# Projection tiles cut into 64-row halves ahead of the attention loop, with five score maxima threaded between them

## The chip, the cores and the metric

The kernel runs on one core of one Trainium2 chip. The metric is the device time of one execution in microseconds; the median of three executions is compared. All tensors are float32, and the matmuls read their operands as float32r.

## The reference

`x` has 2048 rows of 512. It is normalised along its rows, and the normalised rows feed an attention block with 32 heads of 16 columns and a two-layer block with a squared ReLU. The silu of the second gates the first, and `x` is added.

```python
xn  = layernorm(x)                                   # 2048 x 512
qkv = xn @ wqkv                                      # 512 x 1536: q, k, v of 32 heads
p   = softmax(q k^T / 4)                             # per head, 2048 x 2048
s   = (p @ v) @ wo
h   = relu(xn @ w1 + b1) ** 2                        # 1792 columns
out = x + s * silu(h @ w2 + b2)
```

## The kernel before

**Number format.** Every operand is kept as a high and a low part, and a product is three matmuls: high by high, high by low, low by high (`terms3`, L262). A projection tile, 128 by 512 outputs over 512 contracted columns, is therefore 4 pieces of 128 rows times 3, that is 12 matmuls of 128 rows, all adding into one PSUM bank.

**Three stages.** First the layer norm, the transposes of `x`, and the projection tiles of the first heads. Then, from L1109 on, a stage that is called "lead" here: it works off the remaining projection tiles (list `rest`, each entry a generator that `pump` at L1025 advances matmul by matmul) and beside them computes row maxima of the scores. Then the loop (L1332) over 32 units, each four heads by 512 queries, in 16 steps of 128 keys, 512 steps in all. It holds the exponentials, the product with v, the two-layer block, `wo`, and what is left of the maxima.

**Maxima.** The softmax subtracts the maximum of each row of scores. `max_mm(j)` (L288) computes one piece: a matmul of 64 rows (the head's 16 columns are stored as a high, high, low layout within 64 partitions; j is the half of the array, partitions 0 to 63 or 64 to 127) at L300 into a PSUM bank, and a reduction on VectorE at L308 that leaves the maximum of 512 columns. There are 2048 pieces in all, 64 to each of 32 units. Each must be made once, either in the lead or in the loop. Pieces are made by turns on the two halves, since a matmul of 64 rows fills half the array and one on each half run beside each other. In the lead a piece takes its bank alternately from the pool `pe` (tile `se`, three banks) and the pool `pm` (tile `pm_t`, three banks); in the loop from `pm` alone.

**A round of the lead.** L1109 to L1148 run one round for each tile: six pieces of maxima (three on each half), then twelve full matmuls (`pump(12, 1)`). Since `pump(60, 1)` at L1103 stops in the middle of a tile, each twelve are the last eleven of one tile and the first of the next. When a tile is done, ScalarE copies its bank to `raw` (L954) or to `vt` (L971), GpSimd splits `raw` into `hl` (L80, L81), and SyncE stores `hl` to q_d or k_d (L912) in HBM. The tiles' own banks alternate between the single banks of `pd` and `pv` (`q_bank`, L925). `hl` has three buffers and `raw` two. In the same rounds the normalised `x` (xn_d, 1 MB each), keys (ka), queries (qm, qe) and v are moved between HBM and SBUF.

**The order of the work.** The order on TensorE, ScalarE, VectorE and GpSimd is that in which the program issues; TensorE takes its matmuls in that order for both halves. `max_end` (L314) follows the maxima: when 9/16 and 11/16 of a unit's pieces are done it asks for the next unit's queries.

**The loop.** `long_slots` (L1251) runs two steps at a time in a "visit": 12 units of the two-layer block on one half, 8 exponential scores (L1161) and some maxima, and 8 matmuls of 128 rows by 32 columns for the product with v (`pv_mm`, L374), which come four to a step. A visit has two forms. If `ahead_m` (L1241) finds that the maxima are ahead of their due time, it holds 7 maxima and the product of both steps at its end (L1283); otherwise 8 maxima, with the first step's product moved between the tenth and the eleventh unit (L1290, L1295).

```python
                if ahead_m(sum(done_m) + 7, st + 2):
                    visit(h, "s" + "D" * 12 + "s", ".mmsmssmsmssmm")
                    ...
                else:
                    visit(h, "D" * 10, "msmsmsmsms")
```

Of the kernel before, what the change touches and what calls it, by code (L numbers as in the profile page):

```python
# [31 lines left out]
SHIFT = 8  # L32
NVT = 7
# [6 lines left out]
def kernel(  # L40
# [55 lines left out]
    with ExitStack() as ph:  # L96
# [217 lines left out]
        def max_end():  # L314
            while steps[0] < sum(done_m) // 4:
                u, s = divmod(steps[0], 16)
                if s == 15 and min(done_m) < 32 * (u + 1):
                    return
                steps[0] += 1
                if s in (9, 11) and u + 1 < NU:  # L320
                    assert min(done_m) >= 32 * u + 16
# [611 lines left out]
        def qk_tile(m, c, last=False):  # L933
            ps = pd.tile([P, 512], F32, name="pd_t") if last else q_bank()
            for out_, lh, rh, first_, last_ in qk_terms(m, c, ps):
                nc.tensor.matmul(out_, lh(slice(0, P)), rh(slice(0, P)), start=first_, stop=last_)  # L936
                if not last_:
                    yield
            if last:
# [6 lines left out]
                yield  # L946
                return
# [9 lines left out]
            yield  # L957

        def v_tile(c, tt):
            xT = xTs[c]  # L960
            ps = q_bank()
            ts_ = slice(tt * P, (tt + 1) * P)
            for out_, lh, rh, first_, last_ in terms3(ps, [
                (lambda a, q, ko=ko: xT[q, a, ko, ts_], lambda b, q, ko=ko: wa_t[q, b, ko, 2 * P :])
                for ko in range(KO)
            ]):
                nc.tensor.matmul(out_, lh(slice(0, P)), rh(slice(0, P)), start=first_, stop=last_)  # L967
                if not last_:
                    yield
            vt = vts[(4 * c + tt) % NVT]  # L970
            nc.scalar.activation(  # L971
                vt[:, :, :DH], ps.rearrange("p (h d) -> p h d", d=DH), AF.Copy
            )
            nc.sync.dma_start(v_d[:, c * 4 + tt, :], vt.rearrange("p h d -> p (h d)"))
            lead[1] += 1
            yield
# [48 lines left out]
        def pump(n, keep=0):  # L1025
            for _ in range(n):
                while True:
                    todo = ahead or rest
                    if todo is rest and len(rest) <= keep:
                        return  # L1030
                    if next(todo[0], todo) is not todo:
# [25 lines left out]
        for i in range(NT + 3):  # L1057
# [21 lines left out]
            if i >= 3 and (i - 3) % 4 == 3:  # L1079
                c = (i - 3) // 4  # L1080
                ahead.append(qk_tile(4, c))
                (rest if c else ahead).append(qk_tile(0, c))
                rest += [v_tile(c, tt) for tt in range(4)]
# [14 lines left out]
        for n in (2, 3):  # L1098
            fill_ring("ka", n, 1.0)
        rest += [  # L1100
            qk_tile(m, c, (m, c) == (7, 3)) for c in range(4) for m in (1, 5, 2, 6, 3, 7)
        ]
        pump(60, 1)  # L1103
        warm = const.tile([P, 1], F32, name="warm")
# [3 lines left out]
        b = 0  # L1108
        while len(rest) > 1:  # L1109
            now[0] = b - 100  # L1110
            shift_due()
            for _ in range(3):
                for j in range(2):
                    max_mm(j, True)
            pump(12, 1)
# [32 lines left out]
            b += 1  # L1148
        m0[0] = sum(done_m)
# [236 lines left out]
```

## Time and profile before

| what | value |
|---|---|
| median of 3 runs | 1689.39 us (1685.15 to 1689.98) |
| the profiled execution | 1685.93 us |
| its span, first to last instruction | 1684.1 us |
| TensorE busy | 1645.7 us, 98% of the span |
| VectorE busy | 1334.7 us, 79% |
| ScalarE busy | 1190.0 us, 71% |
| first piece of the maxima starts | 64.92 us |
| first exponential score starts (the loop) | 200.11 us |

A matmul's row in the timeline gives its start and a modelled end; matmuls are pipelined, so the time that one takes from the next is the distance of their starts, not the duration. The same holds for VectorE's reductions. A row ahead of which TensorE waited names what ended the wait in brackets. "64*128" in a matmul's row means 64 rows by 128 columns of the array.

### The profile page before, as it was taken

Reading aid. Unit: us, or ns where it says so; the run is one execution under the profiler, and the core shown is the slowest. Engines: PE = TensorE matmul, PEld = TensorE weight load, DVE = VectorE, ACT = ScalarE, POOL = GpSimd, SP = SyncE. Lnnn points to the kernel's source line nnn. Section 1 sums busy time; section 2 is a strip of 40 time slices with the busy share of each in tenths; the row PEclk is TensorE's granted clock in tenths of the full one; section 3 lists DMA queues with packets and bytes.
Section 4 is the critical chain, followed back from the end, with each engine's and each line's share of the span. In section 5 each row is a group of like instructions: output and inputs, shape, how many; then the busy total and the mean of one; then the engine's idle time right before and its main releaser. Section 6 shows DMA issues by size and latency. Waiting matters only on the chain.

```text
span 1684.1 us, 35351 instructions
## 1 busy us (share of the span) xinstructions
PE 1645.7 (98%) x13296; PEld 980.9 (58%) x13296; DVE 1334.7 (79%) x2294; ACT 1190.0 (71%) x2354; POOL 529.2 (31%) x548
## 2 busy tenths in 40 slices
PE   6999999999999999999999999999999999999998
PEld 5766666556655665665566556545655565555533
DVE  6499988887887788777877878888888888888512
ACT  7211277778877777787788777777777777766685
POOL 4424467513311321231133113212221233133333
PEclk9999999999999999999999999999999999999999
DMA  8558465526322533353243324352424332167344
GB/s 282 167 186 258 153 198 157 143 71 158 99 78 78 136 93 84 98 132 80 78 125 114 79 85 117 94 117 68 133 72 108 102 108 67 33 201 213 101 138 134
DMA packets 156723, 208.00 MB, mean 124 GB/s; under 512 B 51272, under 2 KB 71240, under 8 KB 155016
## 3 DMA queue, kind: packets, MB, share of 16 engines
q1 hardware_dynamic: 156552, 205.74, 43.2%
q8 instruction: 105, 1.72, 0.5%
q14 instruction: 66, 0.54, 0.1%
HBM read 149.30 MB, written 56.09 MB: 122 GB/s over the span
## 4 chain that ended last, share of the span: by engine, by line
PE 84%; issue 5%; POOL 4%; DMA 3%; DVE 2%; SPq 1%; ACT 1%; POOLq 0%; ACTq 0%
PE po L374 26%; PE pd_t L234 16%; PE se L1161 14%; PE pm_t L300 13%; PE pd_t L202 5%; PE pd_t L936 2%; PE po L936 2%; DVE mx L308 2%; PE se L300 2%; PE po L967 1%; PE pd_t L967 1%; DMA hl<-r_d 1%; POOL ts L751 1%; POOL ts L750 1%; PE se L936 1%
## 5 line engine op out<-in xcount | busy, mean ns | idle before, releaser
L308 DVE TENSOR_REDUCE mx<-pm_t 128x1 f32<-128x512 f32 x1946 | 1207.3, 683 | 228.7 <-PE pm_t L300 145.3
L1167 ACT ACTIVATE pt<-se 128x512 f32<-128x512 f32 x1721 | 911.6, 614 | 245.0 <-PE se L1161 146.7
L1161 PE MATMUL se<-qe,ka 64*128 64x512 f32 x1988 | 759.5, 420 | 0.1
L300 PE MATMUL pm_t<-ka,qm 64*128 64x512 f32 x1946 | 738.7, 416 | 4.4 <-DVE mx L308 2.7
L374 PE MATMUL po<-pt,v 128*32 128x512 f32 x3562 | 522.2, 602 | 0.0
L300 PEld LDWEIGHTS pm_t<-ka,qm 64*128 64x128 f32 x1946 | 341.8, 184 | 165.7 <-DVE mx L308 150.8
L1161 PEld LDWEIGHTS se<-qe,ka 64*128 64x128 f32 x1988 | 353.2, 184 | 129.8 <-ACT pt L1167 76.8
L234 PE MATMUL pd_t<-xc,w1s 64*128 64x256 f32 x2352 | 318.0, 285 | 0.0
L234 PEld LDWEIGHTS pd_t<-xc,w1s 64*128 64x128 f32 x2352 | 296.8, 187 | 34.6 <-issue 31.8
L234 PE MATMUL pd_t<-w2t,hT 64*128 64x512 f32 x936 | 249.0, 403 | 0.0
L374 PE MATMUL po<-ex,v 128*32 128x512 f32 x534 | 207.9, 601 | 0.0
L1167 ACT ACTIVATE ex<-se 128x512 f32<-128x512 f32 x267 | 159.8, 614 | 46.8 <-PE se L1161 22.7
L234 PEld LDWEIGHTS pd_t<-w2t,hT 64*128 64x128 f32 x936 | 162.4, 185 | 33.9 <-issue 25.1
L374 PEld LDWEIGHTS po<-pt,v 128*32 128x32 f32 x3562 | 90.8, 109 | 155.8 <-issue 138.6
L548 POOL TENSOR_TENSOR r<-r 128x512 f32<-128x512 f32 x49 | 51.0, 1040 | 320.1 <-ACT r L545 320.1
L567 POOL TENSOR_TENSOR u<-u,b_t 128x512 f32<-128x512 f32 x16 | 20.5, 1284 | 283.9 <-ACT u L566 252.2
L202 PE MATMUL pd_t<-w2t,hT 64*128 64x512 f32 x408 | 106.1, 392 | 0.6 <-POOL w2t L81 0.6
L412 POOL TENSOR_TENSOR ot<-ot,hl 128x512 f32<-128x512 f32 x31 | 39.8, 1284 | 211.8 <-DMA hl<-r_d 129.8
L202 PE MATMUL pd_t<-wot,oc 64*128 64x512 f32 x336 | 90.9, 406 | 8.9 <-DVE mx L308 6.2
L202 PEld LDWEIGHTS pd_t<-wot,oc 64*128 64x128 f32 x336 | 58.5, 185 | 57.7 <-ACT pt L1167 16.2
L308 DVE TENSOR_REDUCE mx<-se 128x1 f32<-128x512 f32 x102 | 69.7, 683 | 15.7 <-PE se L300 9.0
L202 PEld LDWEIGHTS pd_t<-w2t,hT 64*128 64x128 f32 x408 | 72.8, 185 | 10.6 <-POOL w2t L81 1.5
(125 smaller groups left out, 1229.2 us busy)
## 6 DMA issues: line engine op xcount, KB each, us to landing
w1s<-w_d SPq DMA_DIRECT2D x196, 256.0 KB
qm<-q_d SPq DMA_DIRECT2D x384, 32.0 KB
qe<-q_d SPq DMA_DIRECT2D x384, 32.0 KB
ka<-k_d SPq DMA_DIRECT2D x96, 128.0 KB
xn_d<-xT SPq DMA_DIRECT2D x8, 1024.0 KB
k_d<-hl SPq DMA_DIRECT2D x32, 256.0 KB
q_d<-hl SPq DMA_DIRECT2D x32, 256.0 KB
xc<-xn_d SPq DMA_DIRECT2D x16, 512.0 KB
```

The costliest lines, as they stand in the source:

```text
L202: mm = nc.tensor.matmul(out_, lh(r), rh(r), start=first_ and lane == 0, stop=last_ and lane == 1, skip_group_check=True,)
L234: mm = nc.tensor.matmul(out_, lh(r), rh(r), start=first_ and lane == 0, stop=last_ and lane == 1, skip_group_check=True,)
L300: nc.tensor.matmul(ps, qms[u][p][64 * j : 64 * j + 64, qb * P : (qb + 1) * P], kas[qd, p][64 * j : 64 * j + 64, kc * 512 : (kc + 1) * 512] ...
L308: return nc.vector.tensor_reduce(mxs[u][:, c, kc : kc + 1], ps, axis=AX.X, op=ALU.max)
L374: nc.tensor.matmul(po[32 * j : 32 * j + 32, :], vs[qd][:, (4 * kb + j) * VW : (4 * kb + j) * VW + 32], pts[j], start=(kb == 0), stop=(kb = ...
L412: nc.gpsimd.tensor_tensor(ot, ot, hl[:, 1].bitcast(F32), op=ALU.mult)
L548: nc.gpsimd.tensor_tensor(r, r, r, op=ALU.mult)
L567: nc.gpsimd.tensor_tensor(u, u, b2_t, op=ALU.add)
L936: nc.tensor.matmul(out_, lh(slice(0, P)), rh(slice(0, P)), start=first_, stop=last_)
L967: nc.tensor.matmul(out_, lh(slice(0, P)), rh(slice(0, P)), start=first_, stop=last_)
L1161: nc.tensor.matmul(se, kas[qd, j // 2][b : b + 64, kb * P : (kb + 1) * P], qes[u][j // 2][b : b + 64, :], start=True, stop=True,)
L1167: return nc.scalar.activation(pts[j], se, AF.Exp, scale=0.25)
```

## The change

Each tile of the lead is issued as two lists: `low`, its 12 matmuls on partitions 0 to 63, and `high`, the same 12 on partitions 64 to 127, both into the same bank. `low` of a tile is issued alternately with what `far` holds at that moment: `far` starts with 23 empty places (15 + LAG), and each tile's `high` is appended to it, so that a tile's second half runs about one tile and eight steps behind its first. Between the twelve of `low` stand two or three maxima of half 0, between those of `high` three or two of half 1: five to a tile where there were six. The empty places of the first two rounds get seven further maxima. After the last tile a tail of steps works off `far`. All maxima of the lead now take their banks from `pm`; the tiles take theirs in turn from `pd`, `pv` and three times `pe`. The first matmul of a second half waits for the reduction of the maximum that ends the first half. The tile that `pump(60, 1)` leaves unfinished is finished, in full matmuls, ahead of the first maximum.

```diff
@@ max_end
+                if s == 11 and min(done_m) < 32 * u + 16:
+                    return
...
         def q_bank():
-            if not lead[0]:
-                return pe.tile([P, 512], F32, name="se")
-            lead[2] += 1
-            if lead[2] % 2:
+            lead[2] += lead[0]
+            if lead[2] % 5 == 1:
                 return pd.tile([P, 512], F32, name="pd_t")
-            return pv.tile([P, 512], F32, name="po")
+            if lead[2] % 5 == 2:
+                return pv.tile([P, 512], F32, name="po")
+            return pe.tile([P, 512], F32, name="se")
...
+        def lead_halves(kind, m, c):
+            ps = q_bank()
+            mms = (v_terms if kind == "v" else qk_terms)(m, c, ps)
+            done = [None]
+
+            def emit(mm, lane, follow):
+                r = slice(64 * lane, 64 * lane + 64)
+                out_, lh, rh, first_, last_ = mm
+                inst = nc.tensor.matmul(
+                    out_, lh(r), rh(r),
+                    start=first_ and lane == 0, stop=last_ and lane == 1,
+                    skip_group_check=True,
+                )
+                if follow:
+                    tc.add_manual_dep(
+                        inst.ins, done[0].ins.name,
...
+                    )
+                if lane and last_:
+                    q_end(kind, m, c, ps)
+
+            def behind(inst):
+                done[0] = inst
+
+            return [
+                [lambda mm=mm, lane=lane: emit(mm, lane, lane and mm is mms[0]) for mm in mms]
+                for lane in range(2)
+            ], behind
...
         pump(60, 1)
+        if not isinstance(rest[0], tuple):
+            for _ in rest.pop(0):
+                pass
...
+        far = [None] * (15 + LAG)
+
+        def step(near):
+            for mine in near:
+                if mine is not None:
+                    mine()
+                if far and far[0] is not None:
+                    far[0]()
+                del far[:1]
+
         while len(rest) > 1:
             now[0] = b - 100
             shift_due()
-            for _ in range(3):
-                for j in range(2):
-                    max_mm(j, True)
-            pump(12, 1)
+            (low, high), behind = lead_halves(*rest.pop(0))
+            low[6:6] = [lambda: max_mm(0)] * (1 + b % 2)
+            low.append(lambda behind=behind: behind(max_mm(0)))
+            high[4:4] = [lambda: max_mm(1)]
+            high[9:9] = [lambda: max_mm(1)]
+            if b % 2 == 0:
+                high.append(lambda: max_mm(1))
+            if b < 2:
+                for i in range(len(far)):
+                    if far[i] is None and i % 5 == 2:
+                        far[i] = lambda: max_mm(1)
+            far += high
+            step(low)
             max_end()
...
+        while far:
+            step([lambda: max_mm(0)] + [None] * 4)
+        max_end()
```

On TensorE, in the middle of the lead (the queries of heads 8 to 15 over the first 512 rows of `x`, the first tile that reads the weights `wr_t`), the program before has a burst of maxima between whole tiles:

```order
L967 MATMUL po<-wa_t,xT_187 128x512 x11
L936 MATMUL pd_t<-xT_188,wr_t 128x512
L300 MATMUL se<-ka_203,qm_202 128x512
L300 MATMUL pm_t<-ka_203,qm_202 128x512
L300 MATMUL se<-ka_203,qm_202 128x512
L300 MATMUL pm_t<-ka_203,qm_202 128x512
L300 MATMUL se<-ka_203,qm_202 128x512
L300 MATMUL pm_t<-ka_203,qm_202 128x512
L936 MATMUL pd_t<-xT_188,wr_t 128x512 x11
```

The same tile (bank `pd_t`) on TensorE in the changed program; a row's shape is that of the output, so the halves read 128x512 as well:

```order
L987 MATMUL se<-wa_t,xT_187 128x512
L987 MATMUL pd_t<-xT_188,wr_t 128x512
L987 MATMUL se<-wa_t,xT_187 128x512
L987 MATMUL pd_t<-xT_188,wr_t 128x512
L301 MATMUL pm_t<-ka_204,qm_201 128x512
L987 MATMUL pd_t<-xT_188,wr_t 128x512
L987 MATMUL se<-wa_t,xT_187 128x512
L987 MATMUL pd_t<-xT_188,wr_t 128x512
L987 MATMUL se<-wa_t,xT_187 128x512
L301 MATMUL pm_t<-ka_204,qm_201 128x512
L987 MATMUL se<-wa_t,xT_187 128x512
L987 MATMUL pd_t<-xT_188,wr_t 128x512
```

Halves of an earlier tile and of this one now alternate, with a single maximum among them here and there, and all maxima name `pm_t`.

In the loop, the end of a visit near step 240 on TensorE, before: the last units of the two-layer block (`pd_t<-xc`), the exponential scores (`se<-qe`), the maxima (`pm_t<-ka`), then the products with v of two steps (`po`) in one run of eight.

```order
L234 MATMUL pd_t<-xc,w1s_2327 128x256 x2
L300 MATMUL pm_t<-ka_203,qm_201 128x512
L234 MATMUL pd_t<-xc,w1s_2327 128x256 x2
L300 MATMUL pm_t<-ka_203,qm_201 128x512
L1161 MATMUL se<-qe_689,ka_685 128x512
L374 MATMUL po<-ex_2307,v_1438 32x512
L374 MATMUL po<-pt_1351,v_1438 32x512
L374 MATMUL po<-pt_1354,v_1438 32x512
L374 MATMUL po<-pt_1343,v_1438 32x512
L374 MATMUL po<-pt_1344,v_1438 32x512
```

At the same place in the changed program:

```order
L235 MATMUL pd_t<-xc,w1s_2632 128x256 x2
L376 MATMUL po<-ex_2610,v_1614 32x512
L376 MATMUL po<-pt_1494,v_1614 32x512
L376 MATMUL po<-pt_1488,v_1614 32x512
L376 MATMUL po<-pt_1490,v_1614 32x512
L235 MATMUL pd_t<-xc,w1s_2632 128x256 x2
L301 MATMUL pm_t<-ka_204,qm_200 128x512
L235 MATMUL pd_t<-xc,w1s_2632 128x256 x2
L301 MATMUL pm_t<-ka_204,qm_200 128x512
L1222 MATMUL se<-qe_688,ka_684 128x512
L1222 MATMUL se<-qe_689,ka_685 128x512 x2
L301 MATMUL pm_t<-ka_204,qm_200 128x512
```

The product of one step has moved into the middle of the block's units: this visit has taken the form with 8 maxima. Counted over the whole order, 27 visits (the 116th to the 142nd pair of steps) change from 7 maxima to 8; the 27 that are missing ahead of the first exponential score, 178 in place of 205, are made up there, and the last maximum stands in the same step as before.

More of the change, by code (lines that the diff above doesn't have):

```diff
@@ L32 @@
 SHIFT = 8
+LAG = 8
 NVT = 7
@@ L1080 @@
                 c = (i - 3) // 4
-                ahead.append(qk_tile(4, c))
-                (rest if c else ahead).append(qk_tile(0, c))
-                rest += [v_tile(c, tt) for tt in range(4)]
+                ahead.append(("qk", 4, c))
+                (rest if c else ahead).append(("qk", 0, c))
+                rest += [("v", tt, c) for tt in range(4)]
         while ahead:
@@ L1100 @@
         rest += [
-            qk_tile(m, c, (m, c) == (7, 3)) for c in range(4) for m in (1, 5, 2, 6, 3, 7)
+            ("qk", m, c) + ((True,) if (m, c) == (7, 3) else ())
+            for c in range(4) for m in (1, 5, 2, 6, 3, 7)
         ]
         pump(60, 1)
+        if not isinstance(rest[0], tuple):
+            for _ in rest.pop(0):
+                pass
         warm = const.tile([P, 1], F32, name="warm")
```

41 lines of the change are left out of this document (22 added, 19 removed).

## The prediction

> **What bounds the kernel now.** I read the page first: it says which engine the span follows.
>
> ```profile
> PE 1645.7 (98%) x13296; PEld 980.9 (58%) x13296; DVE 1334.7 (79%) x2294; ACT 1190.0 (71%) x2354; POOL 529.2 (31%) x548
> ```
>
> TensorE (PE) has work in flight for 98% of the span, VectorE (DVE) for 79%. These are averages over stages with different limits, so the second view is the table by stage, cut at the first maximum (64.92 us) and at the first exponential score (200.11 us).
>
> ```profile
> 64.92:200.11 135.19, 133.53 (x615) 93.08 (x615) 126.32 (x213) 22.42 (x39) 52.76 (x56) 1.00 0.62 199
> 200.11:1600.00 1399.89, 1387.14 (x11997) 817.65 (x12000) 1160.43 (x1959) 1069.94 (x2126) 415.51 (x431) 1.00 0.41 110
> ```
>
> The columns are stretch, length, busy PE, PEld, DVE, ACT and POOL, granted clock, DMA share, GB/s. In the lead (135.19 us) PE and DVE are both nearly full; ScalarE and GpSimd are not; the clock is 1.00, so nothing can come from there. Which of the two sets the pace is seen in one round, in order of time, PE first, then DVE:
>
> ```profile
> 140.52 0.39 PE L936 MATMUL pd_t<-xT,wr_t 128*128 128x512 f32 x1
> 140.83 0.49 PE L300 MATMUL se<-ka,qm 64*128 64x512 f32 x1
> 140.84 0.49 PE L300 MATMUL pm_t<-ka,qm 64*128 64x512 f32 x1
> 141.17 0.39 PE L300 MATMUL se<-ka,qm 64*128 64x512 f32 x1
> ...
> 141.40 0.39 PE L300 MATMUL se<-ka,qm 64*128 64x512 f32 x1
> 141.41 0.39 PE L300 MATMUL pm_t<-ka,qm 64*128 64x512 f32 x1
> 141.72 2.79 PE L936 MATMUL pd_t<-xT,wr_t 128*128 128x512 f32 x11
> 144.35 0.39 PE L936 MATMUL po<-xT,wr_t 128*128 128x512 f32 x1
> 144.67 0.49 PE L300 MATMUL se<-ka,qm 64*128 64x512 f32 x1
> ```
>
> ```profile
> 141.36 0.69 DVE L308 TENSOR_REDUCE mx<-se 128x1 f32<-128x512 f32 x1 [0.16 <-PE pm_t L300]
> 141.97 0.68 DVE L308 TENSOR_REDUCE mx<-pm_t 128x1 f32<-128x512 f32 x1
> ...
> 144.36 0.68 DVE L308 TENSOR_REDUCE mx<-pm_t 128x1 f32<-128x512 f32 x1
> 145.20 0.69 DVE L308 TENSOR_REDUCE mx<-se 128x1 f32<-128x512 f32 x1 [0.16 <-PE pm_t L300]
> ```
>
> The round lasts 144.67 - 140.83 = 3.84 us. A pair of maxima, one on each half of the array, takes as long as one full matmul: 141.40 - 141.17 = 0.23. The eleven full matmuls take 144.35 - 141.72 = 2.63, of which the first takes about 0.34 and the others 0.23. So the round is 15 places of 0.23 (3.45) and about 0.1 extra at each of four **seams**, where the array goes from 128 rows to 64 and back: 140.52 to 140.83 is 0.31, 140.83 to 141.17 is 0.34, 141.41 to 141.72 is 0.31. Together 3.85: PE fills the round without a wait. DVE needs six steps of 0.60 (141.97 to 144.36 is four, 2.39), 3.6 us, and sits idle for the rest, 0.16 of it shown as a wait for PE. **The lead is bound by PE**, with DVE 6% behind it.
>
> **The change part by part: the lead.** A tile becomes 24 halves and 5 maxima, all of 64 rows, so 14.5 pairs instead of 15 places, and the seams go. That holds only if two halves with 512 columns run beside each other as the maxima do. The loop has such pairs (the two-layer block on one half, scores on the other):
>
> ```profile
> 610.38 0.39 PE L234 MATMUL pd_t<-w2t,hT 64*128 64x512 f32 x1
> 610.38 0.39 PE L300 MATMUL pm_t<-ka,qm 64*128 64x512 f32 x1
> 610.61 0.40 PE L234 MATMUL pd_t<-w2t,hT 64*128 64x512 f32 x1
> ...
> 611.99 0.39 PE L234 MATMUL pd_t<-w2t,hT 64*128 64x512 f32 x1
> ...
> 613.07 0.40 PE L234 MATMUL pd_t<-w2t,hT 64*128 64x512 f32 x1
> ```
>
> Seven steps in 611.99 - 610.38 = 1.61 give 0.23; all eleven to 613.07 give 0.245, with waits for other engines in them. I take 0.23 and keep 0.245 as the upper end. The tiles: 33 x 14.5 = 478 steps, and a tail of 24 in which the second half of the last tile is worked off alone: 502 x 0.23 = 115.5 us.
>
> Where it starts:
>
> ```profile
> 63.18 0.86 PE L967 MATMUL se<-wa_t,xT 128*128 128x512 f32 x3
> 64.92 0.46 PE L300 MATMUL se<-ka,qm 64*128 64x512 f32 x1 [0.88 <-DMA ka<-k_d]
> 66.81 0.47 PE L300 MATMUL pm_t<-ka,qm 64*128 64x512 f32 x1 [1.43 <-DMA ka<-k_d]
> ```
>
> Before, PE runs out of projections at about 63.9 and waits for the keys until 66.81. After, the eleven matmuls that are left of the open tile (11 x 0.23 = 2.5) fill that gap; the first maximum comes two steps later, at 66.9. So the steps begin at 66.4, and what was a wait is work that stood behind the burst.
>
> What is added to the 115.5:
>
> ```profile
> 202.54 0.49 PE L300 MATMUL pm_t<-ka,qm 64*128 64x512 f32 x1
> 203.07 1.89 DVE L308 TENSOR_REDUCE mx<-pm_t 128x1 f32<-128x512 f32 x3 [1.14 <-PE se L1161]
> 203.81 0.50 PE L300 MATMUL pm_t<-ka,qm 64*128 64x512 f32 x1 [0.31 <-DVE mx L308]
> 203.82 0.50 PE L1161 MATMUL se<-qe,ka 64*128 64x512 f32 x1
> ```
>
> *Waits for a bank.* All maxima now share three banks. These rows show a bank's turn: 203.81 - 202.54 = 1.27 us from matmul to matmul. The order gives ten maxima in 29 steps, at steps 3, 6, 8, 13, 13, 18, 20, 21, 27, 28; the third one after any stands at least 7 steps (1.6 us) later, and ten reductions take 6.0 of the 6.7 us. Worked through place by place, waits are left in the first two rounds, which hold seven extra maxima (1.6 us), and in the tail (0.7): with the rest 2.5 us. The rows also show what a wait costs: the score on the other half (203.82) starts only with the maximum. By the Trainium skill ("TensorE: Matmul & The Clock Gate", section "Step-by-step: what each phase is for") only weight loads are pulled ahead, and "the MATMULs themselves stay in program order". These rows agree; were it otherwise, the other half would run on, and the 2.5 would be nothing.
>
> *Unit ends.* Two of these fall in the lead, each a transpose for the shift:
>
> ```profile
> L335 PE MATMUL pm_t<-ident,m 128*16 128x128 f32 x4 | 1.1, 272 | 0.0
> ```
>
> At 0.27 and two seams I take 0.5 each, 1.0; a third moves from the lead to the loop (0.5 there).
>
> *Stores.* A tile's evacuation and its stores are unchanged, but come faster (3.34 against 3.84 us, without waits), and with them everything that SyncE issues by rounds: xn_d, keys, queries, v.
>
> ```profile
> 130.00:140.00 10.00, 10.00 (x49) 7.24 (x46) 9.66 (x17) 1.19 (x2) 5.66 (x6) 1.00 0.98 241
> 140.00:150.00 10.00, 9.77 (x45) 6.56 (x45) 9.50 (x17) 1.79 (x3) 4.56 (x6) 1.00 0.91 309
> ```
>
> Here the DMA share is 0.98 and 0.91. A seventh more would not fit into these 20 us; over the whole lead it is 0.62, so it fits a little later. Five banks instead of two in turn cover about two tiles' delay. Bounds: nothing, and 5 us if the 50 us about here (a third of the lead) cannot shrink at all. I take 0.5.
>
> The loop then begins at 66.4 + 115.5 + 2.5 + 1.0 + 0.5 = 185.9 instead of 200.11: **14.2 us less**.
>
> **The loop.** 27 maxima fewer are ready; by the order 27 visits go from 7 to 8 maxima. Four stretches of eight visits each in the first form stand around 841 to 1019 us, where those visits lie, and four in the second from 1109; the table counts reductions:
>
> ```profile
> 841.30:885.60 44.30, 34.36 (x57) 1.00 0.44 121
> 974.60:1019.10 44.50, 34.35 (x57) 1.00 0.28 79
> ...
> 1109.60:1155.70 46.10, 39.79 (x65) 1.00 0.46 107
> 1247.60:1293.60 46.00, 39.78 (x65) 1.00 0.27 63
> ```
>
> 57 reductions go with 44.4 us, 65 with 46.0: (46.0 - 44.4) / 8 = 0.2 a visit, 27 x 0.2 = **5.4 us more**. DVE is 39.8 of 46.0 even there, so it doesn't bind; the price is the second pair of seams around the split product with v.
>
> The sum: -14.2 + 5.4 + 0.5 = **-8.3 us**. Against the profiled execution: 1685.93 - 8.3 = 1677.6. Of the three runs two lie at 1689.4 to 1690.0 and one at 1685.15, so the median stands 3.5 above this execution; taking two thirds of that, I say **1680**.
>
> **The rivals.**
> *The maxima wait at their banks* (slower). Place: the three `pm_t` banks, where six served before. If each maximum is held up, both halves stop and the weights' load comes into the open: 0.49 against 0.39 in the matmul rows above, 0.1 each. Five to a tile in 33 tiles are 16.5 us instead of my 2.5: +5.7, **1695**. It decides from (8.3 + 2.5) / 33 = 0.33 us a tile, 0.065 a maximum. For it: 203.81 shows such a wait of 0.31. Against it: there, three maxima follow within 0.6 us, and here the third after any is 1.6 us away. The Trainium skill ("TensorEngine Tiling (Array Packing)", section "PSUM Bottleneck") says that splitting the array speeds up TensorE but not the evacuation of PSUM, which may become the bound; by that rule DVE would set the lead's pace. The rows here put DVE at 178 x 0.60 = 107 us against 115.5, so close that the rule may hold in places, not on the whole. Chance 0.10.
> *The halves pair less well* (no change). At 0.245 a step the 502 steps cost 7.5 us more: -0.8, **1688**. For it the eleven steps above; against it, their waits are for scores, which the lead hasn't. Chance 0.12.
> *The stores hold the lead* (small gain). With the 5 us of the upper bound: -3.8, **1685**. For it the share of 0.98, against it the slack after. Chance 0.10.
> *The gain is not there since the program doesn't do it*: the order shows the halves alternating, so this is left at nothing.
>
> **How the numbers follow.** My forecast has 0.68: 1680, between 1673 (no waits, no delay of stores, and runs at the level of the profile) and 1684. The rivals have 0.12, 0.10 and 0.10. The range from 1672 to 1688 takes in the two small ones and leaves out the slow one and some of the edges. A measurement of this kernel can tell about 0.3%, 5 us, from no change. Faster by more (below 1684.3): 0.64 of the forecast and 0.05 of the stores' case, 0.69; slower by more: 0.11; the rest, 0.20, within.
>
> **What would show it.** The first exponential score should start near 186 us. Two tiles should take 6.7 us, with starts on each half 0.23 apart, no seam, and DVE at about 90% of the lead. If maxima in the lead show waits for DVE in the middle rounds of more than 0.06 each, the bank rival holds; if steps of 0.245 come without waits, the pairing one; if `raw` waits for GpSimd and that for stores, the third. The loop's stretches between 841 and 1019 should have 65 reductions and 46 us in place of 57 and 44.4. The prediction is wrong in its structure if the loop begins at 186 and the end doesn't follow.

## The result, and the profile after

The changed kernel takes 1676.87 us (median of 4 runs, 1675.25 to 1678.24) against 1689.29 us (4 runs): ratio 0.9931 [0.9913, 0.9949]. In a later group of runs it was 1677.22 (6 runs) against 1685.13 (17 runs), 0.9955 [0.9943, 0.9966]. It is faster, by 0.4 to 0.7%, and the forecast of 1680 within 1672 to 1688 holds. The profiled execution took 1678.24 us, 7.7 less than that of before; the sum said 8.3 less.

The page of the changed kernel, busy time, share and instructions of each engine:

```profile
PE 1638.3 (98%) x13692; PEld 989.4 (59%) x13692; DVE 1336.7 (80%) x2294; ACT 1191.5 (71%) x2354; POOL 529.7 (32%) x548
```

The changed kernel's table by stage, columns as before, cut at the first exponential score (the first maximum comes at 65.94 us, the cut is left at 64.92):

```profile
64.92:185.16 120.24, 119.84 (x978) 107.83 (x976) 109.94 (x182) 22.91 (x39) 52.15 (x56) 1.00 0.68 220
185.16:1600.00 1414.84, 1400.51 (x12070) 814.57 (x12071) 1179.43 (x1993) 1076.32 (x2135) 418.39 (x433) 1.00 0.41 110
```

The shares on the page hardly move: they show nothing of the change. The table does. TensorE is busy for 119.84 of 120.24 us where it was busy for 133.53 of 135.19, with more matmuls (978 for 615) in less time. VectorE went from 126.32 us busy to 109.94, for 182 operations in place of 213, and is at 91% of the stage.

TensorE in the middle of the changed lead, in order of time, with the place at which the lead ends:

```profile
140.63 0.39 PE L987 MATMUL po<-xT,wr_t 64*128 64x512 f32 x1
140.65 0.39 PE L987 MATMUL pd_t<-xT,wr_t 64*128 64x512 f32 x1
140.86 0.39 PE L987 MATMUL po<-xT,wr_t 64*128 64x512 f32 x1
140.87 0.39 PE L987 MATMUL pd_t<-xT,wr_t 64*128 64x512 f32 x1
...
141.34 0.61 PE L301 MATMUL pm_t<-ka,qm 64*128 64x512 f32 x2
...
185.16 0.39 PE L1222 MATMUL se<-qe,ka 64*128 64x512 f32 x1
```

Starts on each half stand 0.23 us apart (140.63 to 140.86, 140.65 to 140.87), and a maximum (141.34) is one of them: no seam is left. The loop begins at 185.16 us instead of 200.11. From there to the end of the span are 1491.28 us instead of 1484.03, so the loop is 7.25 us longer. The lead from its first maximum is 119.2 us instead of 135.2, and the first maximum itself comes 1.0 later.

Waits in the changed lead, three stretches (engine, tile, line, what it waited for: us in total, times, longest), 65 to 80, 80 to 170 and 170 to 185.2 us:

```profile
PEld pm_t L301 <- DVE mx L309: 1.5, 4, 0.4
...
PEld pm_t L301 <- DVE mx L309: 0.8, 5, 0.2
...
PEld pm_t L301 <- DVE mx L309: 0.6, 2, 0.4
```

These sum to 2.9 us, most of it in the first two rounds with their extra maxima and in the tail. In the middle five waits come to 0.8 in 26 tiles. The reductions in the loop's stretches, DVE at L309 (stretch, length, busy and count, clock, DMA share, GB/s):

```profile
871.10:916.80 45.70, 39.65 (x65) 1.00 0.42 111
964.40:1010.10 45.70, 39.82 (x65) 1.00 0.32 83
```

65 reductions take 45.7 us where 57 took 44.4.

### The profile page after: what moved, and what is told of

The parts are those of the page before. It is cut to its first block, busy times and chain, and to the rows that moved or that the text cites. A ratio compares the mean times of both kernels' runs of the same rounds, so it can differ in the third digit from the quotient of the medians.

```text
span 1676.4 us, 36115 instructions
## 1 busy us (share of the span) xinstructions
PE 1638.3 (98%) x13692; PEld 989.4 (59%) x13692; DVE 1336.7 (80%) x2294; ACT 1191.5 (71%) x2354; POOL 529.7 (32%) x548
## 4 chain that ended last, share of the span: by engine, by line
PE 85%; issue 5%; POOL 3%; DMA 3%; DVE 2%; ACT 1%; SPq 0%; POOLq 0%; ACTq 0%; DVEq 0%
PE po L376 26%; PE pd_t L235 16%; PE pm_t L301 15%; PE se L1222 14%; PE pd_t L203 5%; PE se L987 3%; PE se L938 2%; PE pd_t L987 1%; DVE mx L309 1%; PE po L987 1%; POOL ts L753 1%; POOL ts L752 1%; PE pm_t L828 1%; DMA sm<-ot 0%; POOL s L753 0%
## 5 line engine op out<-in xcount | busy, mean ns | idle before, releaser
L309 DVE TENSOR_REDUCE mx<-pm_t 128x1 f32<-128x512 f32 x2048 | 1265.3, 682 | 232.6 <-PE pm_t L301 128.2
L301 PE MATMUL pm_t<-ka,qm 64*128 64x512 f32 x2048 | 780.7, 415 | 4.5 <-DVE mx L309 3.9
L1222 PE MATMUL se<-qe,ka 64*128 64x512 f32 x1988 | 739.1, 415 | 0.0
L376 PE MATMUL po<-pt,v 128*32 128x512 f32 x3560 | 527.7, 603 | 0.0
L301 PEld LDWEIGHTS pm_t<-ka,qm 64*128 64x128 f32 x2048 | 359.8, 184 | 194.2 <-DVE mx L309 181.3
L1222 PEld LDWEIGHTS se<-qe,ka 64*128 64x128 f32 x1988 | 348.9, 184 | 103.0 <-ACT pt L1228 59.8
L235 PEld LDWEIGHTS pd_t<-xc,w1s 64*128 64x128 f32 x2352 | 295.4, 187 | 46.5 <-issue 44.4
L235 PE MATMUL pd_t<-w2t,hT 64*128 64x512 f32 x936 | 252.6, 406 | 0.0
L203 PE MATMUL pd_t<-w2t,hT 64*128 64x512 f32 x408 | 106.4, 392 | 2.0 <-POOL w2t L81 1.2
L82 POOL TENSOR_TENSOR hT<-r,hT 128x512 fp32r<-128x512 f32 x56 | 72.3, 1291 | 4.7
```

The lines of the kernel that those rows point to most:

```text
L82: (lo or nc.gpsimd).tensor_tensor(dst[1], raw, dst[0].bitcast(F32), op=ALU.subtract)
L203: mm = nc.tensor.matmul(out_, lh(r), rh(r), start=first_ and lane == 0, stop=last_ and lane == 1, skip_group_check=True,)
L235: mm = nc.tensor.matmul(out_, lh(r), rh(r), start=first_ and lane == 0, stop=last_ and lane == 1, skip_group_check=True,)
L301: nc.tensor.matmul(ps, qms[u][p][64 * j : 64 * j + 64, qb * P : (qb + 1) * P], kas[qd, p][64 * j : 64 * j + 64, kc * 512 : (kc + 1) * 512] ...
L309: return nc.vector.tensor_reduce(mxs[u][:, c, kc : kc + 1], ps, axis=AX.X, op=ALU.max)
L376: nc.tensor.matmul(po[32 * j : 32 * j + 32, :], vs[qd][:, (4 * kb + j) * VW : (4 * kb + j) * VW + 32], pts[j], start=(kb == 0), stop=(kb = ...
```

## The experiments

The theories, with a letter for each (what an expectation takes up beside them is spelled out there):
- A, the prediction's: the lead is bound by TensorE; its length is places of 0.23 us and seams.
- B: it is bound by VectorE; its length follows the number of reductions ahead of the loop.
- C: the loop's loss doesn't come from the number of maxima that are left for it.
- D: the halves alone bring the gain, wherever the maxima stand among them.
- E, formed after the first four runs: the number of maxima made ahead also sets when SyncE issues the next unit's queries, and the rest of the loop's loss is the crowd that this makes there.
- G: the move of the queries that clears this crowd is a gain of its own, with or without the change.

Four kernels ran on one chip, then four on a second, then four on a third; in each group the kernel before ran beside them with a median of 1685.1 us.

**Five maxima in the kernel before** (`b_five`): bursts of six and four by turns, the tiles whole.

```diff
+                if s == 11 and min(done_m) < 32 * u + 16:
+                    return
...
-            for _ in range(3):
+            for _ in range(3 - b % 2):
```

> The kernel before, with bursts of six and of four maxima by turns: five to a tile as in the change, but whole matmuls and all seams kept. Theory A (TensorE's places and seams set the lead): every second round loses one pair, 17 x 0.23 = 3.9 us, so the loop begins at 196.2 us instead of 200.1; 34 maxima are missing, 34 x 0.2 = 6.8 us more in the loop; in all about 3 us slower than before. Rival B (VectorE's reductions set the lead, and the change gains because there are 27 fewer of them): 34 x 0.6 = 20 us less, the loop begins near 180 us, and the whole is about 13 us faster than before.

Measured: 1692.73 us, 1.0044 [1.0029, 1.0059]. TensorE in `b_five` where the loop begins:

```profile
193.90 0.49 PE L1162 MATMUL se<-qe,ka 64*128 64x512 f32 x1
```

The stretch 80 to 170 us of `b_five` (length, busy PE, PEld, DVE, ACT, POOL, clock, DMA share, GB/s):

```profile
80.00:170.00 90.00, 90.00 (x411) 62.03 (x410) 74.78 (x126) 16.00 (x28) 35.75 (x40) 1.00 0.67 219
```

The loop begins at 193.90, 6.2 earlier, and not near 180. A had 3.9; most of the rest comes from rounds that waited in the kernel before, the one at 148.52 above all (4.77 us), and don't wait here. VectorE is idle for 15 of these 90 us and TensorE for none: with the reductions gone, TensorE set the pace, so B falls. A round with four maxima takes 3.59 us and one with six 3.83: the difference, 0.24, is one pair. The loop lost 13.1 us: 34 visits took the longer form, and there were waits that I had in no theory. Two are for the loads of `xc`, 1.25 and 1.10 us at 207.96 and 209.41, with a granted clock of 0.50 from 210 to 212; by 222 us the loop is 4.4 us behind that of the kernel before. `a_lag5` below shows what the later ones are.

**More seams** (`b_seams`): the same six maxima and the same tile, in two bursts.

```diff
-            for _ in range(3):
-                for j in range(2):
-                    max_mm(j, True)
-            pump(12, 1)
+            for n in (2, 1):
+                for _ in range(n):
+                    for j in range(2):
+                        max_mm(j, True)
+                pump(6, 1)
```

> The kernel before, with each burst of six cut into four and two maxima, six whole matmuls behind each: nothing more to compute, twice as many seams between 128 and 64 rows. Theory A: 0.39 us more in each of 34 rounds, 13 us, the loop begins at 213 us, the whole about 13 us slower. Rival B: the reductions are fewer at a time and better spread, the lead stays as it is or gets shorter by the 0.16 us of idle VectorE in each round, 0 to 5 us faster.

Measured: 1697.08 us, 1.0068 [1.0052, 1.0085]; the lead 11.6 us longer, the loop the same (1483.93 against 1484.03). TensorE in one round:

```profile
142.99 0.49 PE L300 MATMUL se<-ka,qm 64*128 64x512 f32 x1
...
143.32 0.39 PE L300 MATMUL se<-ka,qm 64*128 64x512 f32 x1
...
143.65 1.66 PE L936 MATMUL po<-xT,wr_t 128*128 128x512 f32 x6
145.24 0.50 PE L300 MATMUL se<-ka,qm 64*128 64x512 f32 x1
...
145.67 1.43 PE L936 MATMUL po<-xT,wr_t 128*128 128x512 f32 x5
...
147.25 0.49 PE L300 MATMUL se<-ka,qm 64*128 64x512 f32 x1
```

The round takes 147.25 - 142.99 = 4.26 us where it took 3.84, with not one instruction more: two more passages between the forms of the array cost 0.42, 0.1 for each of their four matmuls. Over the 34 rounds it is 11.6 and not 14, since rounds that waited in the kernel before don't wait here. This is the price that the change removes once a round. The Trainium skill ("TensorEngine Tiling (Array Packing)", section "Key Properties") says that changing the tiling mode drains TensorE; the trace agrees, and this is its size here.

**The open tile finished first** (`b_finish`), in the kernel before.

```diff
         pump(60, 1)
+        pump(11, 1)
```

> The kernel before, with the open tile finished ahead of the first burst, as the change does it, and nothing else: eleven matmuls move into the wait for the keys (2.5 us), and there are 33 bursts instead of 34. If that part of the change is worth what the prediction says, the loop begins 2.5 us earlier, and 1.3 us more for the burst that is gone, at 196.3 us; the six missing maxima cost 1.2 us in the loop; in all 2.6 us faster. If the wait moves along (the keys land later, or their loads were held by something behind the burst), only the burst goes: 198.8 us, and the whole is within 0.3 us of before.

Measured: 1689.28 us, 1.0022 [1.0011, 1.0034]. The expectation miscounted: a finished generator that is left in the list makes a 34th burst, not 33, and it stood right ahead of the loop. What else it cost was new. TensorE in the middle of the lead of `b_finish`:

```profile
148.55 0.50 PE L300 MATMUL se<-ka,qm 64*128 64x512 f32 x1
...
150.12 0.47 PE L300 MATMUL se<-ka,qm 64*128 64x512 f32 x1 [1.07 <-DMA qm<-q_d]
...
151.30 4.61 PE L936 MATMUL po<-xT,wr_t 128*128 128x512 f32 x12
...
155.83 0.50 PE L300 MATMUL se<-ka,qm 64*128 64x512 f32 x1
```

The stretch about it in `b_finish`, columns as above:

```profile
130.00:160.00 30.00, 28.85 (x127) 20.05 (x124) 25.79 (x44) 3.86 (x8) 13.28 (x14) 0.94 0.94 279
```

GpSimd's wait there:

```profile
POOL hl L80 <- DMA q_d<-hl: 8.0, 2, 5.9
```

One round lasts 155.83 - 148.55 = 7.28 us; the same round takes 4.77 in the kernel before (148.52 to 153.29), and most others 3.84. Queries came late, and GpSimd waited 8.0 us in all for the stores of `hl`, at a DMA share of 0.94. The 2.3 us won at the start were lost here. The larger part is not the wait of 1.07 us itself: behind it the granted clock was 0.50 from 152 to 154 us and 0.77 in the next two, and the twelve matmuls took 155.83 - 151.30 = 4.53 us instead of 2.95. The loop is 3.2 us longer too (1487.24), 2.0 of it in its first two visits, right behind the 34th burst, with a clock of 0.68 and 0.50 from 202 to 206 us. So this run doesn't show what the stores cost by themselves. In the changed kernel the same stretch moves nearly as much:

```profile
130.00:160.00 30.00, 30.00 (x259) 26.80 (x257) 27.65 (x47) 5.39 (x9) 18.94 (x20) 1.00 0.83 265
```

GpSimd waits there too (8.3 us for stores to k_d and 4.9 for those to q_d, between 100 and 170 us), and TensorE is busy for 30.00 of 30.00. That the five banks are what takes this up was not tried by itself.

**Five steps of lag in place of eight** (`a_lag5`), in the changed kernel.

```diff
-LAG = 8
+LAG = 5
```

> The change with the second halves five steps behind a tile instead of eight. Theory A with the waits worked out place by place from a bank's turn of 1.27 us and a reduction of 0.60: three steps fewer at the end (0.7 us) and fewer waits in the first two rounds and in the tail (1.5 instead of 2.5 us, as fewer maxima meet there), the loop begins 2.0 us earlier than in the change, at 183.1 us; two maxima fewer cost 0.4 us. In all 1.6 us faster than the change. If the first matmul of a second half had been close to its wait for the reduction, each tile would wait, and the lead would be longer, not shorter, by up to 0.2 us x 33 = 7 us.

Measured: 1683.99 us, 0.9987 [0.9976, 0.9999]. The lead became 2.0 us shorter, as A said. The loop became 7.4 longer than that of the change, and no theory had that. VectorE in `a_lag5`, early in the loop (start, duration):

```profile
248.79 0.25 DVE L400 RECIPROCAL sm<-sm 128x16 f32<-128x16 f32 x1 [2.26 <-DMA sm<-ot]
248.96 1.82 DVE L309 TENSOR_REDUCE mx<-pm_t 128x1 f32<-128x512 f32 x3
```

TensorE at the same place:

```profile
249.64 0.50 PE L301 MATMUL pm_t<-ka,qm 64*128 64x512 f32 x1 [1.39 <-DVE mx L309]
```

The table of `a_lag5` by 2 us, columns as above:

```profile
249.00:251.00 2.00, 1.36 (x9) 0.34 (x9) 2.00 (x5) 0.32 (x1) 1.83 (x5) 1.00 0.93 309
251.00:253.00 2.00, 2.00 (x17) 1.70 (x15) 1.60 (x3) 0.82 (x2) 0.43 (x1) 0.56 0.92 289
253.00:255.00 2.00, 2.00 (x16) 1.36 (x17) 1.26 (x3) 1.47 (x3) 0.00 (x0) 0.59 0.91 292
```

The reciprocal of the softmax sums waits 2.26 us for the sums' transfer. VectorE works in order, so the reductions of the maxima stand behind it, and TensorE waits 1.39 for one of them. Right behind, the granted clock is 0.56 and 0.59 for 4 us. From 255 us on it is 1.00 again. The same comes once more near 397 us: a wait of 1.55 us, and a clock of 0.50 and 0.64 from 398 to 402. A drop takes (1 - 0.56) x 2 + (1 - 0.59) x 2 = 1.7 us of full speed, so by this estimate 3.4 of the 7.4 us are the slower clock behind the waits, and not the waits themselves. What held the transfer is on SyncE. SyncE's queue in the kernel before, early in the loop (start, duration of the issue):

```profile
222.91 3.08 SPq L132 DMA_DIRECT2D qm<-q_d  x6
...
230.40 4.24 SPq L132 DMA_DIRECT2D qm<-q_d  x6
...
245.86 3.28 SPq L132 DMA_DIRECT2D qe<-q_d  x6
...
253.42 2.77 SPq L132 DMA_DIRECT2D qe<-q_d  x6
```

SyncE's queue in `a_lag5`, ahead of the wait above:

```profile
228.81 2.76 SPq L133 DMA_DIRECT2D qm<-q_d  x6
231.68 4.09 SPq L133 DMA_DIRECT2D qe<-q_d  x6
...
237.97 2.81 SPq L133 DMA_DIRECT2D qm<-q_d  x6
240.88 2.67 SPq L133 DMA_DIRECT2D qe<-q_d  x6
243.60 2.04 SPq L369 DMA_DIRECT2D qe<-sh_d  x4
...
246.66 0.61 SPq L394 DMA_DIRECT2D sm<-ot  x1
```

`max_end` asks for the next unit's `qm` at 9/16 and 11/16 of a unit's maxima. Counted from the loop's start, before asks 23 and 30 us into it and `a_lag5` 44 and 53 us, since 29 fewer are ready; the `qe` loads go by the step number and stand at 46 and 53 in the one, 47 and 56 in the other. So each group of six `qm` now has six `qe` right behind it, and behind those stand the sums and the weights `ex`. The diff does not show the order on SyncE. This became theory E.

**Six maxima among the halves** (`a_six`), in the changed kernel.

```diff
-            low[6:6] = [lambda: max_mm(0)] * (1 + b % 2)
+            low[4:4] = [lambda: max_mm(0)]
+            low[9:9] = [lambda: max_mm(0)]
...
-            if b % 2 == 0:
-                high.append(lambda: max_mm(1))
+            high.append(lambda: max_mm(1))
```

> The change with six maxima to a tile instead of five (three in each half, evenly spread): 30 halves and maxima are 15 steps, 3.45 us, but six reductions are 3.6 us. Theory A, worked out place by place: VectorE now sets the pace, the maxima wait 6 us in all at their banks, the loop begins 7.7 us later than in the change, at 192.9 us. About 208 maxima are ready as before the change, so no visit of the loop changes its form and the query loads fall where they fell before: from the loop's begin to the end 1484 us, as before, against 1491 in the change. In all about 1677, the same as the change. Rival C (what the loop lost is not bound to the count of maxima but comes from the earlier start or from the order of halves): the loop keeps its 1491, and the whole is 7 us slower than the change.

Measured: 1679.20 us, 0.9962 [0.9947, 0.9977]. The stretch 80 to 175 us of `a_six`:

```profile
80.00:175.00 95.00, 94.80 (x788) 70.11 (x786) 94.93 (x164) 17.22 (x30) 39.24 (x44) 1.00 0.72 225
```

TensorE's wait in that stretch:

```profile
PEld pm_t L301 <- DVE mx L309: 15.2, 75, 0.3
```

Here VectorE is the bound: busy for 94.93 of 95 us, and TensorE's weight loads wait for it 75 times, 0.2 each. The lead is 6.6 us longer than the change's, the loop back at 1485.26 (1484.03 before). So C falls: the loop's loss goes with the number of maxima left for it. And five to a tile are a trade that comes out nearly even: what they win in the lead they pay in the loop.

**Halves, with the maxima in bursts** (`a_burst`), in the changed kernel.

```diff
-            low[6:6] = [lambda: max_mm(0)] * (1 + b % 2)
+            low += [lambda: max_mm(0)] * (1 + b % 2)
...
-            high[4:4] = [lambda: max_mm(1)]
-            high[9:9] = [lambda: max_mm(1)]
-            if b % 2 == 0:
-                high.append(lambda: max_mm(1))
+            high[6:6] = [lambda: max_mm(1)] * (3 - b % 2)
```

> The change with the maxima of each half in one burst (two or three at the end of the first half, three or two in the middle of the second) instead of spread: the same halves, the same count. Theory A, place by place: the three banks are used up by each burst, the matmuls behind it on both halves wait, 0.6 us a tile; the lead is 18.7 us longer than in the change, the loop begins at 203.8 us, later than before the change. The whole near 1696. Rival D (the halves alone are the gain, where the maxima stand doesn't matter): the loop begins at 185 to 188 us.

Measured: 1697.30 us, 1.0067 [1.0051, 1.0084]; the lead 20.4 us longer than the change's, the loop the same (1491.08). TensorE's wait from 80 to 190 us:

```profile
PEld pm_t L301 <- DVE mx L309: 22.3, 54, 0.6
```

Same matmuls, same count of maxima, no seams either, and slower than before: D falls. Without spacing, a maximum finds its bank unread, and both halves stop.

**Two steps of lag** (`a_lag2`), in the changed kernel: the second half's first matmul, which waits for a reduction (`follow`), comes sooner.

```diff
-LAG = 8
+LAG = 2
```

> The change with second halves two steps behind a tile instead of eight. Theory A, place by place: the maximum that ends a first half stands four steps (0.9 us) ahead of the first matmul of the second half, and its reduction needs 1.2 us or more, so each tile waits for it on both halves, 0.6 us a tile: the lead is 18 us longer than in the change, the loop begins near 203.5 us. If the wait on that reduction didn't matter, the loop would begin six steps earlier, 1.4 us, at 183.8 us.

Measured: 1705.31 us, 1.0121 [1.0107, 1.0136]; the lead 18.7 longer than the change's. TensorE's waits from 80 to 190 us:

```profile
PEld se L987 <- DVE mx L309: 13.7, 17, 0.9
PEld pd_t L987 <- DVE mx L309: 4.2, 5, 0.9
PEld po L987 <- DVE mx L309: 3.6, 5, 0.9
```

The waiting tiles are now the projection's own banks: 21.5 us in 27 waits, one to nearly every tile. Eight steps of lag hide the wait that the change adds; five do too, two don't. The loop of the profiled execution is another 10.7 us longer than the change's (1501.91), which the expectation did not have. As in `a_lag5`, VectorE waits 10.8 us for the sums, and near 270 and 420 us the granted clock falls to 0.50.

**The reciprocal later** (`a_lag5_recip`): the sums have two steps more before VectorE asks for them.

```diff
-LAG = 8
+LAG = 5
...
-EVAC = (1, 4, 5, 7, 9, 12)
+EVAC = (1, 6, 7, 9, 11, 13)
```

> The change with second halves five steps behind (whose loop took 1498.7 us against 1491.3 in the change), and the reciprocal of a unit's sums asked for two steps later (6 instead of 4 behind the unit's end, and what hangs on it behind that). Theory E: VectorE takes its work in order, and the reciprocal waits there for the transfer of the sums, which the query loads have pushed back on SyncE; the maxima behind it are late, and TensorE with them. Then the two waits of TensorE on VectorE near 250 and 397 us (1.4 and 1.5 us, and the lower clock behind them) go, the one at 296 us (2.5 us, for the weights w2t) stays: 3 to 5 us off the loop, 1494 to 1496. Rival F (the wait of the reciprocal is hidden, the slower clock comes of itself): the loop stays at 1498 to 1499.

Measured: 1681.00 us, 0.9970 [0.9959, 0.9982]. VectorE's idle time ahead of the reciprocal over the whole run (us, times), in `a_lag5`:

```profile
  DMA sm<-ot: 10.8, 5
```

The same in `a_lag5_recip`:

```profile
  DMA sm<-ot: 0.6, 1
```

The wait is all but gone, and the loop of the profiled execution is 5.8 us shorter (1492.92): F falls. The profile flatters it: this execution is the fastest of its six, and the medians, on two chips, lie only 1683.99 - 1681.00 = 3.0 apart. TensorE still waits 2.5 and 0.8 us for `w2t`, whose `ex` stands in the same queue. So the sums are a part of the crowd's cost and not all of it; which part is the larger, the profile and the medians answer differently.

**The queries' loads apart** (`a_lag5_qe`): `qe` four steps later, so that it doesn't follow `qm` at once.

```diff
-LAG = 8
+LAG = 5
...
-            if 2 <= u < NU and s < 2:
-                load_q_pair(u, "qe", s, qes.setdefault(u, []))
+            if 2 <= u < NU and 4 <= s < 6:
+                load_q_pair(u, "qe", s - 4, qes.setdefault(u, []))
...
-                later(max(2, 16 * u - 14 - now[0]), back)
+                later(max(2, 16 * u - 10 - now[0]), back)
```

> The change with second halves five steps behind, and the twelve loads of the next unit's queries for the exponentials (qe) four steps later in each unit, away from the loads for the maxima (qm), which the smaller count of maxima has moved to the end of a unit. Theory E: it is the crowd on SyncE at the unit's end, 24 loads of 0.47 us each in a row, that holds back the sums and the loads of w2; without it all three waits of TensorE go (249, 296, 397 us): 6 to 8 us off the loop, 1490 to 1492, and 1675 to 1677 in all. If the new place only moves the crowd onto the reciprocals and the shift rows, the loop stays within 2 us of 1498.7 or gets longer.

Measured: 1673.45 us, 0.9927 [0.9912, 0.9942]. The same kernel ran again on another chip as `best`, beside the change and beside the same move in the kernel before.

> The change with second halves five steps behind and the qe loads four steps later, as run before (1673.5 us), beside the change on one chip. Theory E: 2 us from the lead, 4 us from the loop (waits for w2t and for VectorE behind the sums), 0.4 us back for two maxima: 4 to 6 us faster than the change.

> The change itself once more, on the chip of the runs beside it, so that it is compared with them there. All theories: the loop begins at 185.2 us within 1.5 (the first stage moves by that much), about 11 us faster than before on the same chip, near 1677.

Measured: `best` 1674.20 us (1673.55 to 1674.33), 0.9932 [0.9920, 0.9944], and the change 1677.22 (1676.04 to 1680.29), 0.9955 [0.9943, 0.9966]. SyncE's queue in `best`, at the place shown for `a_lag5`:

```profile
238.13 2.76 SPq L133 DMA_DIRECT2D qm<-q_d  x6
...
241.93 0.57 SPq L394 DMA_DIRECT2D sm<-ot  x1
...
243.15 2.77 SPq L133 DMA_DIRECT2D qe<-q_d  x6
```

The sums are issued at 241.93 instead of 246.66, ahead of the `qe` loads and not behind them. The loop is 1487.44 us, 11.2 less than with the same lag and the loads together, and VectorE never waits for the sums. By the medians `a_lag5_qe` is 10.5 below `a_lag5`. This is the fastest kernel of the study: 3.0 us below the change on the same chip, where 4 to 6 were expected. The change with the loads apart and its own lag of eight was not run.

**The same move in the kernel before** (`b_qe`).

```diff
-            if 2 <= u < NU and s < 2:
-                load_q_pair(u, "qe", s, qes.setdefault(u, []))
+            if 2 <= u < NU and 4 <= s < 6:
+                load_q_pair(u, "qe", s - 4, qes.setdefault(u, []))
...
-                later(max(2, 16 * u - 14 - now[0]), back)
+                later(max(2, 16 * u - 10 - now[0]), back)
```

> The kernel before with the qe loads four steps later in each unit and nothing else. Theory E: before the change the loads for the maxima stood in the middle of a unit, so there is no crowd to undo; the reciprocal's two waits (4.0 us on VectorE, of which TensorE saw 1 to 2) may go: 0 to 2 us faster, and the qe loads are not a gain by themselves. Rival G (the new place of the qe loads is simply better, whatever the count of maxima): 6 us faster or more, as with the change at five steps.

Measured: 1682.99 us, 0.9993 [0.9976, 1.0010]; in the profile the loop is 3.2 us shorter (1480.79). By the interval this is not to be told from no change, but one execution alone at 1697.86 widens it: the ten others that it counts lie between 1681.40 and 1685.19, and their mean, 1682.8, is 2.7 us below that of the kernel before (1685.6). So the move is probably a small gain by itself, of about 3 us, where E had 0 to 2 and G 6 or more. G falls as the explanation of the 11.2 us: most of the crowd is made by the change in the maxima, with or without halves, as `b_five` had it too (9.3 us of idle VectorE at the sums, 4.0 in the kernel before).

## Why the prediction was right, and where a term was off

*The lead is bound by TensorE.* Right: `b_five` and `b_seams` move it by places and by seams. VectorE was named as 6% behind, and that was near the truth too: one maximum more per tile, and it takes over (`a_six`).

*The halves pair at 0.23.* Right: starts of 0.23 in the rows; five tiles take 16.67 to 17.42 us in the five turns of the bank `pd_t`, 3.40 a tile, so 6.8 for two against 6.7 forecast. The rival at 0.245 a step falls.

*Waits for a bank, 2.5.* Measured 2.9, in the places named. The rival in which they cost 16.5 falls for the change, but `a_burst` (22.3 us) and `a_lag2` (21.5) show its mechanism: the matmuls of the other half do not run on past the one that waits. The forecast said that of the score at 203.82. What the Trainium skill says of PSUM's evacuation as the bound ("TensorEngine Tiling (Array Packing)", section "PSUM Bottleneck"), which stood behind that rival, holds as it was weighed: not at five maxima to a tile, fully at six (`a_six`).

*Stores, 0.5.* GpSimd waited for them as the rival said, and TensorE didn't wait for GpSimd. That rival falls for the change. In `b_finish` such waits stand beside late queries and a lower clock, so it isn't shown there that stores alone can decide.

*The loop begins at 185.9.* Measured 185.16. Its start came a little sooner than in the sum (first maximum at 65.94, not 66.9), and the length was 119.2 against 119.0. On the profiles the lead gave 14.95 us, 0.75 more than forecast.

*The loop, +5.4 and +0.5.* Measured +7.25: this is the term that was mis-sized. Where it was lost is seen by counting the loop's 2048 score matmuls (`se<-qe`), eight to a visit. Score n is the n-th after the first one. The 27 visits that change their form lie between score 896 and score 1184 (numbers 116 to 144, counted from nought, without two that had 8 maxima already). Score 896 comes at 831.79 and score 1184 at 1032.72 in the kernel before, at 817.59 and 1024.91 in the change: 207.32 us instead of 200.92. So these visits cost 6.4 us, 0.24 each, where I had 0.2 from the 57 and 65 reductions. `best` and `b_qe`, two kernels without the crowd, agree: they differ by 29 maxima and by 1487.45 - 1480.79 = 6.66 us in the loop, 0.23 a visit. Ahead of score 896 the change lost 0.8 us, and behind score 1184 0.1.

The 0.8 is what is left of two larger parts, both of which I had at nothing. One is that fewer maxima ahead shift SyncE's loads. The change shows it in GpSimd's row for the weights of the two-layer block:

```profile
292.82 0.62 POOL L81 TENSOR_SCALAR w2t<-ex 128x512 fp32r<-128x512 f32 x1 [8.10 <-DMA ex<-in_B_w_dram]
```

Behind it TensorE waits 1.2 and 0.8 us (293.50 and 294.85), 2.0 that before doesn't have there; at score 512 the change is 2.4 us behind. The other is a wait of the kernel before for the sums of a later unit:

```profile
582.92 0.25 DVE L398 RECIPROCAL sm<-sm 128x16 f32<-128x16 f32 x1 [2.84 <-DMA sm<-ot]
```

There TensorE waits 1.14 us for a maximum behind it (583.77), and the change does not: it makes up 1.7 us between scores 512 and 544. So of the 2 us that the crowd costs the change most is made up there, and the mis-sized price of a visit is the largest part of the error. By luck this error and the one in the lead nearly cancel: -7.7 in place of -8.3.

*The level of the runs.* I added 2.4 to the profiled time, since the three runs shown lay above it. That step failed: the changed kernel's median is 1.4 below its profiled execution, and the kernel before has a median of 1685.1 in three later groups of 9 to 19 runs. Three runs say little of a level that differs by 4 us; the profile's own time was the better base. On record an execution's time tends to go with its mean granted clock (of the group of 19, the shortest, 1683.0 us, has 0.999, the longest, 1689.4, 0.996), and drops like the one in `a_lag5`, 1.7 us each, come in some executions and not in others.

## What to carry to other kernels

Matmuls of 64 rows are a filler for one another: where full matmuls alternate with half-height ones, cutting the full ones in two removes the drains and gives each small matmul a place, but only if a lag and a spacing between the small ones hide their banks' turn; in bursts the same cut lost 0.7%. Whatever counts work done to decide when to issue loads moves with the amount of work done, so list every queue that hangs on such a count before saying that an edit touches one stage. When a change moves a bound, try the neighbouring numbers (five or six maxima, lag five or eight) with the side effect taken away, since it can hide which is better: lag five looked worse by 7 us until the loads were apart.

## What the runs showed of the hardware

Waits of one to two microseconds on TensorE were followed by some 4 us at about half clock, in some executions only. In `a_lag5` TensorE was busy for 1.25 us of the 2.00 from 247 on and for 1.36 of the next 2.00, which hold a wait of 1.39; the granted clock was then 0.56 to 0.59 for 4 us (251 to 255 us). The Trainium skill ("TensorE: Matmul & The Clock Gate", section "What's actually happening") gives an idle window of some 3.4 us ahead of half speed; the drop to about half agrees, while here the one wait before it was less than half as long. The change was profiled twice (`after_again` on another chip), and both executions have the same two waits: 1.17 and 0.85 us at 293.50 and 294.85, and 1.16 and 0.86 at 293.71 and 295.07. The first kept a granted clock of 1.00, the second fell to 0.50 right behind them (`after`, then `after_again`):

```profile
296.00:298.00 2.00, 2.00 (x20) 1.32 (x14) 1.58 (x5) 0.94 (x3) 1.92 (x3) 1.00 0.46 169
296.00:298.00 2.00, 2.00 (x10) 0.20 (x8) 0.98 (x3) 0.53 (x1) 1.91 (x3) 0.50 0.55 158
```

So the length of a wait does not decide by itself whether the clock falls; what else decides is not shown here. A single profiled execution can be off by such a drop.

Small loads are dear for the engine that issues them: six of 32 KB occupy SyncE for 2.7 to 4.2 us, as the rows for `qm` and `qe` show, so the 24 of one unit take 12 us (2.76, 4.09, 2.81 and 2.67 in `a_lag5`) in which nothing else of its queue gets out. The price goes by the load more than by its size: the issue of one `ex` of 256 KB takes 0.38 us in the same queue (237.54 in `a_lag5`).
